# One core, attention then a squared-ReLU layer: the last queries' scores move into the half-row run, P.V joins the layers' PSUM ring, and more units of layer 1 are done by seven products

## The chip, the core and the metric

The kernel runs on one core of a Trainium2 chip. The time is the device time of the whole program in microseconds, one launch. A run of the kernel can also be profiled: the profile gives the span from the first to the last instruction, and the start and duration of every instruction on each engine. The engines are TensorE (PE; its weight loads are PEld), VectorE (DVE), ScalarE (ACT), GpSimd (POOL) and SyncE (SP, which here only issues DMAs). Each follows its own list of instructions, in the program's order, and they meet by semaphores.

## The reference

Inputs: q, k, v of 8 batches, 8 heads, 576 positions, 64 dimensions each; a table of 32 distance buckets by 8 heads; w_in (512 x 2048) and w_out (2048 x 512). All float32.

```
scores = q @ k^T / 8 + bias[bucket(|i - j|), head]       # per batch and head
attn   = softmax(scores)                                  # over the keys
x      = (attn @ v), heads side by side                   # 4608 tokens x 512
out    = (relu(x @ w_in) ** 2) @ w_out                    # 4608 x 512
```

From a distance of 128 on the bucket is the same, so the bias is a constant there, which drops out of the softmax; the kernel multiplies only a band around the diagonal by exp(bias).

## The kernel before, in words

**Work and staging.** A pair is two heads of one batch: 32 pairs. Their transposed queries and keys lie in `qt` and `kt` (fp16), head 0 of the pair on partitions 0 to 63, head 1 on 64 to 127. Positions 0 to 511 are four tiles of 128; 512 to 575 are the last 64. `pair` (from line 902) does a pair:

- The main scores, `run` (line 962): for each key tile `jt` and each head a product of 64 rows (the head's dimensions) by 512 queries into a bank of its own of the set `st` (two banks, one per head). Head 0 uses the upper half of TensorE's rows, head 1 the lower half; these are the products of line 971. Two sets exist (`r_set`), and ACT takes the exponential of a whole set (line 984, 1024 elements) into `pt`.
- The last keys, `last_keys` (line 1014): the 64 last keys of both heads against all queries. The keys of the two heads are spread into a zeroed block of 128 by 128 (`kz`), so that one full-row product serves both heads (line 1022).
- The last queries, `last_queries` (line 989): the 64 last queries of both heads spread in the same way into `qz` by four copies per pair (line 954, on POOL, in the first batches partly DVE); four full-row products of 128 columns, one for each key tile (line 997; line 854 in batch 0), into half a set, and one exponential of 512 elements (line 1007; 864).
- DVE multiplies the bands (line 710), then P.V in `values` (from line 722): per query tile one product with the last keys (line 736) and eight of 65 columns (line 743), into the single bank of the ring `r_pv`; DVE takes reciprocals and scales (757, 762), and SP transposes the result by DMA into `xt` (line 777). In batches 0 and 1 TensorE does that transposing (line 1089).

Batch 0 is done by halves of the queries (`half_of_pair`, line 788; scores at line 809, exponentials at 819, last keys at 832 and 841) so that layers can start early.

**Layers.** Tokens go in nine groups of 512. Layer 1 of a group is 16 blocks of 128 of w_in's columns: four products of 512 columns each (line 1486; in group 0 by halves of the tokens, line 1439), a ReLU on ACT (1515) and a square on DVE (1525). Layer 2 (`second`) is done for every group by seven products of blocks in place of eight (Strassen's way, line 1215); DVE makes the sums of activations (1170) and fuses the evacuations of the products (1243), ACT copies some (1249), SP stores (1271). For some blocks of layer 1 `by_sevens` does the same: a unit is four of the 16 blocks at once, seven products of four matmuls of 256 columns (line 1370), evacuated by ACT (1401) for products 1 and 2 and by fused additions on DVE (1396) for the other five, with ReLU (1410) and square (1419 on ACT or 1421 on DVE). It needs sums of w_in (per unit) and of x (per group), made by DVE in `late_sums` (line 1296). The sums of w_in are put in a `pt` buffer, `late["room"]`, that the attention no longer uses. `UNITS` says how many units a group has: one in group 7, two in group 8.

**PSUM.** Eight banks: two sets of two (`r_set`), one for P.V (`r_pv`), three for the rest (`r_g`: layers, transposes, tables). A use takes a buffer from a ring and gives it back when its last reader is done.

**Order.** The order is not that of the code. Each step is an `Op` with engine, cost, inputs, buffers and a due time; `Plan.schedule` (lines 187 to 270) places at each moment the op that can start first, and among those the one due first. The table `DUES` overwrites due times by an op's number, so it holds for one list of ops only. `mode` is "r" for the half-row runs, "c" for the transposes of line 927 and "f" for full-row work; the planner charges TensorE for a change of mode.

Of the kernel before, what the change touches and what calls it, by code (L numbers as in the profile page):

```python
# [22 lines left out]
HQ = 288  # L23
# [17 lines left out]
SIX = 2  # L41
V_EARLY, V_HW = 18900.0, 2
LATE2 = 7000
UNITS = {7: 1, 8: 2}
# [22 lines left out]
0:6314 10:217026 16:13035 20:13348 21:258484 25:16976 56:-3806 60:10549 64:7807 66:10391 72:10797 74:9599  # L67
80:12958 82:13335 86:9426 88:22059 90:20784 96:15474 98:18110 100:27635 102:17069 104:20413 106:19133 108:15929
110:20294 112:11373 114:26373 118:23163 120:26863 122:27399 124:27420 126:43949 128:373644 130:37551 132:55933
140:51535 146:53249 148:57194 150:58550 152:59093 154:59407 156:62212 158:60024 162:61598 164:73576 166:62626  # L70
168:69684 170:59456 172:62632 174:65227 176:55548 182:127159 185:61268 197:113382 198:91426 200:94475 202:78241
204:62718 208:77636 228:78221 232:79984 234:88997 236:93444 258:97082 260:107098 264:95693 272:353255 290:132179
294:109389 312:161034 317:126634 462:185572 468:197791 498:216177 504:216419 528:-11357 540:58268 548:290781
552:-273 556:362102 569:117287 570:18693 572:322613 573:269880 577:216286 580:63789 588:19830 590:16140
594:14836 595:13461 604:192461 605:259149 615:250357 618:40193 621:36476 626:164336 627:19259 631:22289
632:61824 637:27216 640:23193 641:22984 642:25439 646:24359 648:23862 654:35487 655:137994 656:25970 657:147534
658:26859 669:32802 670:29693 671:29115 675:26812 678:61416 684:27758 687:32723 692:45873 693:44475 694:33461
700:29155 703:40767 706:43870 707:156896 712:138157 715:49177 721:51431 727:42451 730:41204 733:51304 736:188811
739:160633 741:60556 745:65841 746:65543 750:23359 752:198955 754:252034 755:87356 757:149452 759:161491
764:165691 772:38120 780:31226 786:44132 789:65256 791:41900 794:47703 798:179998 803:183900 804:201524  # L80
806:29768 808:32093 814:128297 817:38985 819:48235 822:13166 831:74297 834:41254 836:42214 847:56558 872:76658
876:81357 881:86779 885:82175 890:132194 892:78033 896:74640 901:77029 905:85179 910:92737 913:136934 921:-441
928:71969 932:86010 949:99012 964:77998 968:82501 971:73188 973:72043 979:88379 993:74328 994:172863 1011:91462
1016:95167 1034:90187 1037:94214 1061:98210 1066:103404 1085:116705 1089:123193 1094:115422 1098:123870
1105:125413 1109:116922 1114:123206 1117:104913 1118:108524 1126:215561 1127:140015 1134:341379 1138:129625
1149:123522 1156:126934 1159:128458 1174:117297 1178:116128 1183:123079 1184:121785 1193:130123 1197:131687
1210:103421 1213:171180 1215:111597 1218:107124 1224:123395 1234:97893 1238:106935 1239:113870 1242:121817
1245:107498 1247:139583 1250:140247 1256:140312 1264:152762 1302:164129 1307:159578 1311:156509 1314:140955
1322:175554 1327:174839 1336:155878 1340:158933 1342:162590 1347:179715 1351:176523 1358:154680 1362:174863
1365:164726 1369:178450 1372:164377 1375:183307 1391:148354 1396:141354 1405:158959 1423:158387 1426:145359  # L90
1428:154083 1460:162604 1493:305936 1511:188689 1515:208724 1518:185439 1520:203719 1524:203903 1527:183718
1531:64671 1534:35571 1535:192349 1540:192734 1544:215992 1547:197129 1549:206804 1552:201055 1553:198295
1560:216382 1567:22170 1571:213455 1575:214781 1579:220037 1582:216714 1585:209292 1589:218699 1604:51306
1609:177927 1612:165312 1615:244855 1616:185704 1636:180272 1639:191978 1641:180694 1668:199141 1673:209138
1676:207232 1684:113822 1687:219314 1700:201270 1701:203032 1703:191761 1708:195625 1724:230338 1733:225496
1736:226874 1737:226114 1740:65884 1747:238275 1753:233568 1762:229606 1766:238797 1773:230961 1777:231038
1784:245369 1788:237869 1795:246877 1798:236767 1817:211479 1818:211996 1836:232334 1849:219048 1852:216620
1854:244560 1857:216881 1881:227052 1884:224715 1886:230825 1887:234567 1889:218551 1895:248220 1896:246247
1916:239890 1932:255715 1937:245391 1946:276466 1950:271723 1957:144182 1961:262946 1966:264120 1969:283402
1970:252823 1973:283834 1975:263020 1986:281169 1997:277541 2001:273225 2008:269557 2011:263820 2030:290375  # L100
2033:300439 2035:288262 2038:298147 2070:215597 2094:283860 2099:280265 2140:278987 2160:322023 2175:327834
2187:203430 2191:314100 2194:95297 2196:320960 2200:327640 2205:312307 2209:311170 2216:306662 2220:44915
2227:316413 2231:323176 2238:310309 2241:322560 2256:323083 2258:322318 2260:298171 2281:330645 2283:323528
2290:323454 2298:283980 2316:319108 2342:324427 2349:318937
# [146 lines left out]
def mm(n):  # L251
    return n / 2.4 + 2.5
# [11 lines left out]
def kernel(  # L264
# [44 lines left out]
    z_sb = sb("qz", [128, NQK, 2, 128])  # L309
    qzs, kzs = ([z_sb[:, i, w, :] for i in range(NQK)] for w in range(2))  # L310
# [19 lines left out]
    pv_ps = [psum.tile([128, 512], FP32, name=f"pv{i}") for i in range(1)]  # L330
    g_ps = [psum.tile([128, 512], FP32, name=f"f{i}") for i in range(3)]

    P = Plan()
    r_set, r_pv, r_g, r_lane = Ring(2), Ring(1), Ring(3), Ring(8)
# [136 lines left out]
    z_fix = [[fill(zz[:, 0], 0.0, 158.0, 10, QUIET)], [fill(zz[:, 1:], 0.0, 452.0, 11, LATER)]]  # L471
# [316 lines left out]

    def half_of_pair(p, part, turned):
# [10 lines left out]
        def scores(jt):  # L800
            st = Buf(r_set)

            def score():
                kt, qt = kts[qb.slot], qts[qb.slot]
                for j in range(2):
                    for e in range(2):
                        rw = ds(64 * e, 64)
                        io(
                            nc.tensor.matmul(  # L809
                                sets_ps[st.slot][:, e, ts(j, 256)], kt[rw, ts(jt + j, 128)], qt[rw, ds(q0, 256)],  # L810
                                start=True, stop=True,
                            )
                        )

            o = P.add({"PE": 2 * mm(256) + 10}, score, evac + ready, [st, qb, pb], T, 0.0, "r")

            def ex():
                io(
# [3 lines left out]
                    )  # L822
                )

            exps[jt] = P.add({"ACT": act(1024)}, ex, [o], [st, pb], T)

        def last_keys():
            st = Buf(r_g)
# [47 lines left out]
        if part:  # L876
            last_queries()
# [716 lines left out]
```

## Time and profile before

| | us |
|---|---|
| runs without profile | 365.94, 365.03, 367.13; median 365.94 |
| the profiled execution's own time | 365.5 |
| its span, first to last instruction | 363.7 |
| TensorE clock granted, mean | 1.00 |
| main scores, exponentials (ACT L984, L819) | 108.6 and 16.9 busy |
| last queries: products (L997, L854) | 10.7 and 1.6 busy, 128 matmuls |
| last queries: exponentials (L1007, L864) | 17.2 and 3.2 busy, 32 instructions |
| copies into qz and kz on POOL (L954) | 19.7 and 19.9 busy, 56 each |
| layer 1 in full blocks (L1486) | 113.8 busy, 592 matmuls |
| layer 1 by seven products (L1370) | 84 matmuls of 256 columns, 273 ns each |
| fused evacuations of these (DVE L1396) | 15 instructions, about 686 ns each |

A busy time is the union of the durations on an engine; a matmul's duration includes its way through the array, so that matmuls in sequence overlap, and what one takes of the stream is the distance from its start to the next start. In a group row of the profile the columns are line, engine, operation, out<-in, shape, count, busy time and mean ns. A row of TensorE's wait list is: who waited, for whom, total us, times, longest us. In a timeline row: start in us, duration in us of what is merged in the row, engine, line, operation, out<-in, shape, count.

### The profile page before, as it was taken

Reading aid. Unit: us, or ns where it says so; the run is one execution under the profiler, and the core shown is the slowest. Engines: PE = TensorE matmul, PEld = TensorE weight load, DVE = VectorE, ACT = ScalarE, POOL = GpSimd, SP = SyncE. Lnnn points to the kernel's source line nnn. Section 1 sums busy time; section 2 is a strip of 40 time slices with the busy share of each in tenths; the row PEclk is TensorE's granted clock in tenths of the full one; section 3 lists DMA queues with packets and bytes.
Section 4 is the critical chain, followed back from the end, with each engine's and each line's share of the span. In section 5 each row is a group of like instructions: output and inputs, shape, how many; then the busy total and the mean of one; then the engine's idle time right before and its main releaser. Section 6 shows DMA issues by size and latency. Waiting matters only on the chain.

```text
span 363.7 us, 10232 instructions
## 1 busy us (share of the span) xinstructions
PE 352.8 (97%) x4062; PEld 252.7 (69%) x4062; DVE 269.7 (74%) x622; ACT 260.1 (72%) x385; POOL 187.9 (52%) x345
## 2 busy tenths in 40 slices
PE   3989999999999999999999999999999999999996
PEld 2658787765687457777776566458777788566885
DVE  4889999767965598467687589558767685489683
ACT  4999998489866897588968787884685741667530
POOL 7998489979999989856777773012000000000000
PEclk9999999999999999999999999999999999999999
DMA  9999999999999999999999997234320132000032
GB/s 169 137 159 198 201 165 189 123 159 185 148 150 170 212 168 171 136 174 161 146 142 154 176 113 93 65 62 72 105 63 3 50 78 78 29 29 2 31 116 89
DMA packets 162256, 44.29 MB, mean 122 GB/s; under 512 B 145664, under 2 KB 162208, under 8 KB 162208
## 3 DMA queue, kind: packets, MB, share of 16 engines
q0 software_dynamic: 74208, 14.53, 51.4%
q1 hardware_dynamic: 87696, 28.80, 44.2%
q8 instruction: 32, 0.52, 0.6%
q10 hardware_dynamic: 304, 0.31, 0.3%
q14 instruction: 16, 0.13, 0.1%
HBM read 36.89 MB, written 9.44 MB: 127 GB/s over the span
## 4 chain that ended last, share of the span: by engine, by line
PE 92%; ACT 2%; DVE 0%; issue 0%
PE f L1215 30%; PE f L1486 28%; PE pv L743 10%; PE st L971 8%; PE f L1439 4%; PE pv L736 3%; PE st L1022 2%; PE st L997 2%; ACT pt L819 2%; PE st L1370 1%; PE pv L1370 1%; PE f L1089 1%; PE f L927 1%; PE pv L1215 0%; PE f L1370 0%; PE st L809 0%
## 5 line engine op out<-in xcount | busy, mean ns | idle before, releaser
L984 ACT ACTIVATE pt<-st 128x1024 f16<-128x1024 f32 x112 | 108.6, 1024 | 24.6 <-PE st L971 24.6
L1486 PE MATMUL f<-xt,w_in_sb 128*128 128x512 f16 (+4 forms) x592 | 113.8, 333 | 0.0
L1515 ACT ACTIVATE rt<-f 128x512 f16<-128x512 f32 x116 | 68.2, 606 | 31.6 <-PE f L1486 28.4
L1486 PEld LDWEIGHTS <-w_in_sb 128*128 128x128 f16 x592 | 51.8, 98 | 42.4 <-issue 9.8
L710 DVE TENSOR_TENSOR pt<-pt,tb_sb 128x512 f16<-128x512 f16 (+3 forms) x108 | 61.3, 580 | 18.1 <-ACT pt L984 16.5
L1525 DVE TENSOR_TENSOR g<-rt 128x512 f16<-128x512 f16 x116 | 50.6, 442 | 26.5 <-ACT rt L1515 25.0
L1215 PEld LDWEIGHTS <-g 128*128 128x128 f16 x576 | 54.6, 98 | 9.0 <-issue 2.1
L349 POOL DMA_DIRECT2D ks<-in_k_dram x79 | 55.9, 722 | 3.7 <-issue 1.2
L349 POOL DMA_DIRECT2D qs<-in_q_dram x79 | 55.5, 711 | 2.4 <-DMA qt<-qs 1.9
L743 PE MATMUL pv<-va,pt 128*128 128x65 f16 x1280 | 54.6, 193 | 0.0
L743 PEld LDWEIGHTS <-pt 128*128 128x128 f16 x1280 | 50.2, 97 | 2.0
L1215 PEld LDWEIGHTS <-s 128*128 128x128 f16 x432 | 40.8, 98 | 9.4 <-issue 4.2
L1243 DVE SCALAR_TENSOR_TENSOR y<-f,y 128x512 f32<-128x512 f32 (+1 forms) x47 | 31.3, 665 | 18.9 <-PE f L1215 16.8
L954 POOL COPY qz<-qt 64x64 f16<-64x64 f16 x56 | 19.7, 351 | 40.3 <-DMA qt<-qs 34.9
L1215 PE MATMUL f<-wt,g 128*128 128x256 f16 x288 | 36.2, 273 | 0.0
L1215 PE MATMUL f<-w_out_sb,s 128*128 128x256 f16 x288 | 35.8, 273 | 0.0
L736 PE MATMUL pv<-vm,pm 128*128 128x130 f16 x160 | 35.5, 222 | 0.0
L971 PE MATMUL st<-qt,kt 64*128 64x512 f16 x224 | 33.9, 381 | 0.0
L1215 PE MATMUL f<-w_out_sb,g 128*128 128x256 f16 x272 | 33.3, 273 | 0.0
L762 DVE TENSOR_TENSOR x<-pv,r 128x384 f16<-128x384 f32 (+1 forms) x64 | 31.1, 487 | 1.1
L954 POOL COPY qz<-kt 64x64 f16<-64x64 f16 x56 | 19.9, 356 | 10.4 <-DMA kt<-ks 4.8
L1170 DVE TENSOR_TENSOR s<-g,s 128x1024 f16<-128x1024 f16 x36 | 24.9, 697 | 0.1
(101 smaller groups left out, 412.2 us busy)
## 6 DMA issues: line engine op xcount, KB each, us to landing
out_dram<-y SPq DMA_DIRECT2D x34, 256.0 KB, 2.7
f<-in_v_dram SPq DMA_DIRECT2D x24, 256.0 KB, 4.6
ks<-in_k_dram POOLq DMA_DIRECT2D x48, 64.0 KB, 5.2
qs<-in_q_dram POOLq DMA_DIRECT2D x48, 64.0 KB, 4.7
w_in_sb<-in_moe_w_in_dram POOLq DMA_DIRECT2D x4, 512.0 KB, 8.7
w_out_sb<-in_moe_w_out_dram POOLq DMA_DIRECT2D x4, 512.0 KB, 13.0
ks<-in_k_dram POOLq DMA_DIRECT2D x7, 144.0 KB, 5.0
qs<-in_q_dram POOLq DMA_DIRECT2D x7, 144.0 KB, 4.8
```

The source lines that it names most:

```text
L349: lambda: io(eng.dma_start(out=out_(), in_=in_())),
L710: io(nc.vector.tensor_tensor(out=a, in0=a, in1=t, op=MULT))
L736: nc.tensor.matmul(ps[:, i, :, :], pm[:, c : c + 128], vm[:, hp, :, 0:65], start=True, stop=False)
L743: nc.tensor.matmul(ps[:, i, e, :], pt[:, (2 * jt + e) * S + c : (2 * jt + e) * S + c + 128], va[:, jt, 2 * hp + e, 0:65], start=False, sto ...
L954: io(eng.tensor_copy(out=dst[qb.slot][rw, rw], in_=src[qb.slot][rw, 512:576]))
L971: nc.tensor.matmul(sets_ps[st.slot][:, e, :], kt[rw, ts(jt, 128)], qt[rw, 0:512], start=True, stop=True,)
L984: nc.scalar.activation(out=p5(pts[pb.slot])[:, jt, :, 0:512], in_=sets_ps[st.slot], func=EXPF, scale=SCALE)
L1215: nc.tensor.matmul(home[bf.slot][:, ts(s_, HALF)], left(c, s_), right(c), start=(c == 0 and (s_ == 0 or apart) and (own or i not in before ...
L1243: nc.vector.scalar_tensor_tensor(out=dst, in0=ps, scalar=OSC, in1=ys[y[plus].slot][:, cs], op0=MULT, op1=mybir.AluOpType.add,)
L1486: nc.tensor.matmul(g_ps[bank.slot][:, a:z], w_in_sb[:, kk, ts(nt, 128)], xt_sb[:, kk, c : c + z - a], start=(kk == 0), stop=(kk == 3),)
L1515: io(nc.scalar.activation(out=rts[rb.slot], in_=g_ps[bank.slot], func=RELUF))
L1525: nc.vector.tensor_tensor(out=gs[gb1.slot][:, nt, :], in0=rts[rb.slot], in1=rts[rb.slot], op=MULT)
```

## The change

The last queries' scores are no longer four full-row products. `scores_of` puts them into the half-row run of the last key tiles (`run(..., True)`; in batch 0 the second half's `scores(2, True)`): eight products of 64 columns on half the rows, four for head 0 ahead of the large products, four for head 1 behind them, each head into a bank of its own from the ring `r_g`. Within the run head 1 now comes before head 0. `exp_of_last` takes two exponentials of 256 elements. `qz` and its copies are gone. The P.V bank joins the three others: `r_pv` is `r_g`, a ring of four banks. `UNITS` becomes three units in group 7 and four in group 8, so `by_sevens` uses two rooms. The table of due times is new throughout, so the order changes everywhere; among the first instructions SP now issues the bucket table before id and q, the cast of q is done by ACT, not DVE, and the small table product stands before the first transposes. In the changed program the lines are moved: half-row products 801 (64 columns) and 810, their exponentials 820 and 986 (853 in batch 0), P.V 740 and 747, layer 2 1193, seven products 1348, full blocks 1464.

```diff
--- before.py
+++ after.py
@@ -41,7 +41,7 @@
-UNITS = {7: 1, 8: 2}
+UNITS = {7: 3, 8: 4}
...
@@ -306,8 +310,8 @@
-    z_sb = sb("qz", [128, NQK, 2, 128])
-    qzs, kzs = ([z_sb[:, i, w, :] for i in range(NQK)] for w in range(2))
+    z_sb = sb("kz", [128, NQK, 128])
+    kzs = [z_sb[:, i, :] for i in range(NQK)]
@@ -327,11 +331,11 @@
-    pv_ps = [psum.tile([128, 512], FP32, name=f"pv{i}") for i in range(1)]
-    g_ps = [psum.tile([128, 512], FP32, name=f"f{i}") for i in range(3)]
+    g_ps = pv_ps = [psum.tile([128, 512], FP32, name=f"f{i}") for i in range(4)]
...
-    r_set, r_pv, r_g, r_lane = Ring(2), Ring(1), Ring(3), Ring(8)
+    r_set, r_g, r_lane = Ring(2), Ring(4), Ring(8)
+    r_pv = r_g
@@ -468,7 +472,7 @@
-    z_fix = [[fill(zz[:, 0], 0.0, 158.0, 10, QUIET)], [fill(zz[:, 1:], 0.0, 452.0, 11, LATER)]]
+    z_fix = [[fill(zz[:, 0], 0.0, 110.0, 10, QUIET)], [fill(zz[:, 1:], 0.0, 270.0, 11, LATER)]]
@@ -786,6 +790,42 @@
                 xt_ready.setdefault(g_, []).append(t)
         return o
 
+    def scores_of(slot, banks, jts, q0, n, lq):
+
+        kt, qt = kts[slot], qts[slot]
+        rw = [ds(64 * e, 64) for e in range(2)]
+
+        def last(e):
+            for j in range(4 if lq else 0):
+                io(
+                    nc.tensor.matmul(
+                        lq[e][:, ts(j, 64)], kt[rw[e], ts(j, 128)], qt[rw[e], 512:S], start=True, stop=True
+                    )
+                )
+
+        last(0)
+        for i, jt in enumerate(jts):
+            for e in (1, 0):
+                io(
+                    nc.tensor.matmul(
+                        banks[i][:, e, :], kt[rw[e], ts(jt, 128)], qt[rw[e], ds(q0, n)], start=True, stop=True
+                    )
+                )
+        last(1)
+
+    def exp_of_last(lq, pb, o, T):
+
+        def ex(e):
+            io(
+                nc.scalar.activation(
+                    out=p5(pts[pb.slot])[:, :, e, 512:S],
+                    in_=g_ps[lq[e].slot][:, 0:256].rearrange("p (j s) -> p j s", j=4),
+                    func=EXPF, scale=SCALE,
+                )
+            )
+
+        return [P.add({"ACT": act(256)}, lambda e=e: ex(e), [o], [lq[e], pb], T) for e in range(2)]
+
     def half_of_pair(p, part, turned):
 
         hp = p % 4
@@ -797,22 +837,16 @@
...
-        def scores(jt):
+        def scores(jt, last=False):
             st = Buf(r_set)
+            lq = [Buf(r_g) for _ in range(2)] if last else []
 
             def score():
-                kt, qt = kts[qb.slot], qts[qb.slot]
...
-            o = P.add({"PE": 2 * mm(256) + 10}, score, evac + ready, [st, qb, pb], T, 0.0, "r")
+                banks = [sets_ps[st.slot][:, :, ts(j, 256)] for j in range(2)]
+                scores_of(qb.slot, banks, [jt, jt + 1], q0, 256, [g_ps[x.slot] for x in lq])
+
+            took = 2 * mm(256) + 10 + (4 * mm(64) if last else 0)
+            o = P.add({"PE": took}, score, evac + ready, [st, qb, pb] + lq, T, 0.0, "r")
...
             exps[jt] = P.add({"ACT": act(1024)}, ex, [o], [st, pb], T)
+            if last:
+                exps["q"], exps["q1"] = exp_of_last(lq, pb, o, T)
@@ -834,7 +870,7 @@
-            o = P.add({"PE": mm(nk)}, score, evac + ready + spread[2:4], [st, qb, pb], T, 0.0, "f")
+            o = P.add({"PE": mm(nk)}, score, evac + ready + spread, [st, qb, pb], T, 0.0, "f")
@@ -845,36 +881,9 @@
...
         scores(0)
         last_keys()
-        scores(2)
-        if part:
-            last_queries()
+        scores(2, part == 1)
@@ -945,7 +954,7 @@
-        for w, src, dst in ((0, qts, qzs), (1, kts, kzs)):
+        for w, src, dst in ((1, kts, kzs),):
@@ -959,22 +968,15 @@
-        def run(jts):
+        def run(jts, last=False):
             sets = [Buf(r_set) for _ in jts]
+            lq = [Buf(r_g) for _ in range(2)] if last else []
 
             def score():
-                kt, qt = kts[qb.slot], qts[qb.slot]
...
-            o = P.add({"PE": len(jts) * mm(512) + 10}, score, evac, sets + [qb, pb], T, after, "r")
+                scores_of(qb.slot, [sets_ps[st.slot] for st in sets], jts, 0, 512, [g_ps[x.slot] for x in lq])
+
+            took = len(jts) * mm(512) + 10 + (4 * mm(64) if last else 0)
+            o = P.add({"PE": took}, score, evac, sets + [qb, pb] + lq, T, after, "r")
@@ -987,31 +989,8 @@
...
-        def last_queries():
-            st = Buf(r_set)
...
-                    io(
-                        nc.tensor.matmul(
-                            sets_ps[st.slot][:, 0, ts(jt, 128)], kts[qb.slot][:, ts(jt, 128)], qzs[qb.slot],
...
-            o = P.add({"PE": 4 * mm(128)}, score, evac + spread[0:2], [st, qb, pb], T, after, "f")
...
-            exps["q"] = P.add({"ACT": act(512)}, ex, [o], [st, pb], T)
+            if last:
+                exps["q"], exps["q1"] = exp_of_last(lq, pb, o, T)
-            o = P.add({"PE": 2 * mm(HQ)}, score, evac + spread[2:4], [st, qb, pb], T, after, "f")
+            o = P.add({"PE": 2 * mm(HQ)}, score, evac + spread, [st, qb, pb], T, after, "f")
@@ -1042,12 +1021,11 @@
             run([1])
             last_keys()
             run([2])
-            run([3])
+            run([3], True)
         else:
             run([0, 1])
             last_keys()
-            run([2, 3])
-        last_queries()
+            run([2, 3], True)
@@ -1063,7 +1041,7 @@
-                [exps[3], exps["q"]] + tabs_done[0:5], [pb], T,
+                [exps[3], exps["q"], exps["q1"]] + tabs_done[0:5], [pb], T,
@@ -1285,7 +1263,8 @@
     late = {}
 
     def sum_of_w(i, u):
-        return pts[late["room"].slot][:, ts(i - 1, 1024)].rearrange("p (k c) -> p k c", k=2)[:, :, ts(u, 256)]
+        room = pts[late["room", u // 2].slot][:, ts(i - 1, 1024)]
+        return room.rearrange("p (k c) -> p k c", k=2)[:, :, ts(u % 2, 256)]
 
     def late_sums(n, dst, terms, deps, due, bufs=()):
 
@@ -1303,10 +1282,9 @@
 
     def by_sevens(g, units, due):
 
-        assert max(UNITS.values()) <= 2
-        if not late:
-
-            late["room"] = Buf(r_pt)
+        for u in range(units):
+            if ("room", u // 2) not in late:
+                late["room", u // 2] = Buf(r_pt)
         c = (g * GT) % XR
         assert c + GT <= XR
         wq = lambda i, k, u: w_in_sb[:, 2 * k : 2 * k + 2, 1024 * i + 256 * u : 1024 * i + 256 * u + 256]
@@ -1335,7 +1313,7 @@
                         (4, (lambda u=u: wq(0, 1, u), lambda s_=s_: s_(2), SUB)),
                         (3, (lambda u=u: wq(0, 0, u), lambda u=u: wq(1, 0, u), SUB)),
                     ],
-                    l_win + last_scores, due + 10.0 * u, [late["room"]],
+                    l_win + last_scores, due + 10.0 * u, [late["room", u // 2]],
                 )
             banks = {"a": Buf(r_set), "b": Buf(r_g), "c": Buf(r_pv), "d": Buf(r_set)}
             y = {"u": Buf(r_f), "v": Buf(r_y)}
```

The table `DUES` (some 40 lines of numbers) is replaced as a whole and is not shown.

## The prediction

> **What bounds the kernel now.** I read the page first, then the list of what TensorE waited for, then its timeline, to price one instruction of each kind. The page's busy time and its slices:
>
> ```profile
> PE 352.8 (97%) x4062; PEld 252.7 (69%) x4062; DVE 269.7 (74%) x622; ACT 260.1 (72%) x385; POOL 187.9 (52%) x345
> PE   3989999999999999999999999999999999999996
> ACT  4999998489866897588968787884685741667530
> ```
>
> TensorE is full from the fourth slice on; ScalarE (ACT) is full only in slices 2 to 6. The waits of TensorE, all but one more of 0.3 us (L809, for DVE's kt):
>
> ```profile
> PE f L927 <- ACT ks L551: 5.2, 1, 5.2
> PE st L809 <- ACT pt L819: 1.0, 3, 0.5
> PE f L401 <- DMA g<-c_rep: 0.9, 1, 0.9
> PE st L809 <- ACT qt L696: 0.3, 1, 0.3
> ```
>
> The lines are all of the start (L809 is batch 0). After 28.7 us nothing is waited for, so there a change is worth what it does to TensorE's own stream, as long as it makes no new wait. Busy time overlaps, so the stream is priced by starts, in the timeline (start, duration):
>
> ```profile
> 76.72 1.03 PE L1486 MATMUL f<-xt,w_in_sb 128*128 128x512 f16 x4
> 77.67 0.61 PE L971 MATMUL st<-qt,kt 64*128 64x512 f16 x4
> 78.21 1.90 PE L1486 MATMUL f<-xt,w_in_sb 128*128 128x512 f16 x8
> ...
> 86.97 0.41 PE L743 MATMUL pv<-va,pt 128*128 128x65 f16 x8
> 87.21 0.22 PE L736 MATMUL pv<-vm,pm 128*128 128x130 f16 x1
> ...
> 90.62 0.39 PE L997 MATMUL st<-qz,kt 128*128 128x128 f16 x4
> 90.85 1.03 PE L1486 MATMUL f<-xt,w_in_sb 128*128 128x512 f16 x4
> ```
>
> and later, around the one seven-product group:
>
> ```profile
> 319.08 0.60 PE L1370 MATMUL f<-ks,pt 128*128 128x256 f16 x4
> 319.52 1.89 PE L1486 MATMUL f<-xt,w_in_sb 128*128 128x512 f16 x8
> 321.25 0.60 PE L1370 MATMUL f<-ks,pt 128*128 128x256 f16 x4
> ```
>
> From start to start: 128x512 costs 216 ns ((321.25-319.52)/8), 256 columns 109 ns, 128 columns 56 ns (0.23/4), the 65-column products of P.V 30 ns (0.24/8). A run on half the rows (L971) does 4x512 two by two, so 432 ns of streaming, in 0.54 us: about 0.1 us is lost at its end, and 0.09 at its start (0.95 for 4x216=864 ns before it). I take 97 ns per switch between the half-row and full-row forms. Adding these prices over the program's order gives 347.2 us; the profile's time minus this sum is 11.6 us at 29.7 us and 13.3 at the end: fill at the start, then 1.7 us of rounding, no stall. The span is 11.6 + 347.2 + 1.7 + 3.2 (tail: last evacuation and store). The profiled execution took 365.5 us (span 363.7), 0.4 below the shown median of 365.94.
>
> **Last queries.** The 4 products of 128 columns per pair (L997, L854) go: 128 x 56 = 7.2 us. In come 8 of 64 columns per pair, inside the last half-row run: four for head 0 first, then the large ones, head 1 before head 0, then four for head 1. No row shows 64 columns on half the rows. Nearest is L743, 65 columns with a new weight load each, 30 ns; I take 29. What a pair then costs depends on whether head 1's 512-column product may start while head 0's four are still queued. The Trainium skill speaks with two voices. Its page "TensorEngine Tiling (Array Packing)", Tiling Modes, says that different tiles execute loads and matmuls in parallel; then only 4x29 = 117 ns are added, as both halves carry equal work. Its page "TensorE: Matmul & The Clock Gate", Part 3, says that matmuls start and end strictly in program order; then head 1's product starts only with head 0's fourth, 87 ns late, and its own four come after at 4x29: 204 ns added. The row (L971, heads issued in turn) allows both. I take the in-order reading, as the timeline shows no start out of order: 32 x 204 = 6.5 us in, 7.2 out, -0.6 us; side by side it would be 3.7 in, -3.4 us.
>
> A rule of the Trainium skill speaks against short products: "TensorEngine Tiling (Array Packing)", Instruction Overhead, gives each matmul some 60 cycles. Read as added to the stream it is 25 ns on top of 27, 52 a piece, and 7x52 = 364 ns per pair: +4.5 us. The L743 row, 30 ns for 65 columns, says that it isn't added. I keep 29.
>
> ScalarE gets two exponentials of 256 elements for one of 512. Rows of batch 0:
>
> ```profile
> 15.77 0.41 ACT L841 ACTIVATE pm<-f 128x256 f16<-128x256 f32 x1
> 16.03 0.69 ACT L696 ACTIVATE kt<-f 128x576 f16<-128x576 f16 x1
> ...
> 23.35 0.78 ACT L864 ACTIVATE pt<-f 128x512 f16<-128x512 f32 x1
> 23.83 3.05 ACT L819 ACTIVATE pt<-st 128x1024 f16<-128x1024 f32 x3
> ```
>
> Start to start 0.26 against 0.48 us: +0.05 per pair, 1.6 us in all, hidden behind TensorE after the start (ACT is 72% busy); uncovered it would cost 1.6. The qz copies (64, mostly POOL at 0.35 us) and half the zero fill go at no gain on the path: only ACT's exponentials waited for qz, and TensorE did not wait for ACT. POOL's loads may run earlier; nothing waits for them.
>
> **Switches.** Counted in both built programs' orders, form changes on TensorE go from 154 to 149: 5 x 97 = -0.5 us.
>
> **Seven products.** Four more units: 64 products of 512 columns go (13.8 us), 112 of 256 come (12.2): -1.6 us, if TensorE stays the bound there. The stage before:
>
> ```profile
> 290.00:335.00 45.00, 45.00 (x382) 32.52 (x379) 33.01 (x71) 22.68 (x39) 0.00 (x0) 1.00 0.16 45
> ```
>
> The columns after TensorE and its loads are DVE 33.0 and ACT 22.7 of 45 us. In the new order, from the first of the seven units to product 1 of the last layer-2 group TensorE's stream is 39.7 us. DVE has 35 fused evacuations in it (5 a unit, 0.605 start to start in L1396), 16 sums and stores of layer 2 at 0.60 and 6 short ones at 0.34: 32.8 us. ACT has 35 copies and ReLUs (0.49 to 0.52) and 26 squares (0.53) with two copies more: 32.6 us. Both fit, with 7 us to spare, but each engine takes its instructions in the program's order, so I laid out this stage's DVE queue instruction by instruction against TensorE's sum (0.2 us from a product to its evacuation): every bank is free 0.3 to 0.6 us before its next product; the last squares land 0.35 us before product 1 of the last group. No stall, little margin; ends for the cost: -0 and +3 us. The 8 extra sums of w_in (8 x 0.34 on DVE) stand in front of that stage beside TensorE's layer 2, and so do the input's DMA transposes, which DVE's sums wait for; the last must be issued by SP behind two stores, and I find it landing some 2 us early.
>
> **Ring of four.** P.V, layer 1, layer 2 and the last queries now share four banks. In the order, the nearest reuse of a bank after last queries is 0.98 us of TensorE work later, the chain that frees it (end of the product 0.16, hand-over 0.04, exponential 0.43, hand-over 0.05) 0.68. Cost 0; bounds under rivals.
>
> **Start.** SP now loads q last, and q's cast moves to ACT behind the table's exponential; the table product stands before the first transposes, so TensorE begins with the wait for c_rep (6.7 us) in place of the one at 5.2. Following the queues, the first large exponential still starts near 10.6 us (10.73 before), as casts, tables and evacuations held it. From there ACT is the bound until the last batch-0 scores: its rows sum to 20.6 us up to the exponential that frees the set for the next last-keys product, so 31.2 us, where TensorE's sum stands at 20.6. Profile time less sum is then 10.6, against 11.8 before at that place (35.8 us). I count -0.7 of these -1.1, for small gaps on ACT; ends -1.5 and +1.0 (q's landing decides).
>
> **Sum.** -0.6 - 0.5 - 1.6 - 0.7 = -3.4 us: 362.1 against the profiled 365.5, 362.5 against the median.
>
> **Rivals.** (A) as summed, 362.5, chance 0.48. (B) The two halves run side by side: 2.8 us more gained, 359.7, chance 0.25. For it: the Tiling page, and that loads of both heads start 2 ns apart; against: the in-order rule. (C) ACT or DVE falls behind in the seven-product stage or early batches, 2 to 4.5 us of waits: about 365.7, no change, 0.14. For: ACT and DVE at 82% there, margins of 0.3 us; against: the same tightness caused no wait before. (D) Slower: a bank wait at the head of the last-queries run. Head 0's bank must be free before the first product, and behind it in TensorE's queue stand the large scores that feed ACT. If an ACT instruction (0.49 us) lies between, the run waits for it; at half of 32 runs that is 7.8 us: 370.3. It decides from a mean wait of 0.11 us per pair (gain gone), 0.16 for slower by 0.5%. For: three such waits in the start's L809 lines; against: none later. 0.09. (E) Short products at 52 ns: 367.6, 0.04; even at 44 ns.
>
> **Numbers.** Faster by over 0.5% (about what a measurement of this kernel can tell from no change, 1.8 us): A, B and a little of C, 0.75; within: 0.14; slower: 0.11. Range 358.9 to 366.2: from B with its better start to the middle of C; D, E and C's end stay out.
>
> **What would show it.** Last-queries lines of TensorE: the first large product of the run 90 ns after the first short one, and the short tail after it, show A; at once shows B. TensorE's waits after 30 us should be empty; an entry with "ACT pt" or "DVE x" at the short products shows D, one at the seven-product line C. DVE in 290 to 330 us near 85%. TensorE's 36 us mark should lie about 1 us deeper in its work. Wrong if the start's first exponential comes over 1 us late.

## The result, and the profile after

The changed kernel takes 363.68 us (median of 8 runs, 362.59 to 364.83), the kernel before 365.86 in the same set: ratio 0.9937, interval 0.992 to 0.9955, so 2.2 us less where 3.4 were forecast. Two later sets gave 0.9893 (0.9852 to 0.9934) and 0.9935 (0.9905 to 0.9965). The profiled execution took 364.48 us with a span of 362.7, 0.8 above its median; that of before took 365.5 with 363.7. The page's row of busy times and TensorE's slices, after the change:

```profile
PE 348.1 (96%) x4238; PEld 261.1 (72%) x4238; DVE 276.7 (76%) x624; ACT 271.1 (75%) x435; POOL 173.3 (48%) x293
PE   2887999999999999999999999999999999999996
```

TensorE is full later than before: its first four slices read 2, 8, 8, 7 where they read 3, 9, 8, 9. The list of its waits after the change:

```profile
PE f L405 <- DMA g<-c_rep: 6.9, 1, 6.9
PE st L810 <- DVE kt L702: 1.1, 1, 1.1
PE f L801 <- DVE qt L702: 0.9, 1, 0.9
PE f L1417 <- DMA w_in_sb<-in_moe_w_in_dram: 0.9, 1, 0.9
PE f L747 <- DMA va<-in_v_dram: 0.6, 1, 0.6
PE f L740 <- ACT pt L820: 0.4, 1, 0.4
...
PE f L1193 <- ACT y L1227: 0.2, 1, 0.2
```

All but the last lie before 36 us (left out is one of 0.3 us, there too). The last is a wait for a bank of the new ring: at 60.2 us a product of layer 2 stands until ACT has emptied a bank (it reads nothing that ACT writes). A second one, at 144.6 us (P.V, until DVE has emptied a bank), is too short for the list. By the starts they cost 0.22 and 0.25 us. Rival C's waits in the seven-product stage would show at L1348 and rival D's, all through, at L801; there are none. C's other place, the early batches, does have waits: 1.1 and 0.9 us at L810 and L801 for DVE, and 0.4 us at L740 for ACT's short exponentials. The last-queries run, in the timeline of TensorE:

```profile
172.77 0.20 PE L801 MATMUL f<-qt,kt 64*128 64x64 f16 x1
172.78 0.39 PE L810 MATMUL st<-qt,kt 64*128 64x512 f16 x1
172.81 0.25 PE L801 MATMUL f<-qt,kt 64*128 64x64 f16 x3
172.89 0.59 PE L810 MATMUL st<-qt,kt 64*128 64x512 f16 x3
173.22 0.28 PE L801 MATMUL f<-qt,kt 64*128 64x64 f16 x4
173.43 0.23 PE L740 MATMUL f<-vm,pm 128*128 128x130 f16 x1
```

Head 1's large product starts 13 ns after head 0's first short one, although three short ones stand ahead of it in the program; they start after it. Only the second four, at the end, take time. From the run's start to the next full-row product it is 665 ns (median), where a run of four large products takes 538: +126 ns a pair with rounding. That is rival B. The stage of the seven products, to be set beside the row from 290 us on that the prediction shows (columns: window, length, then busy time and instructions of TensorE, its loads, DVE, ACT, POOL, then clock and DMA):

```profile
290.00:335.00 45.00, 45.00 (x443) 39.02 (x441) 40.79 (x80) 29.24 (x53) 0.00 (x0) 1.00 0.18 54
```

DVE is at 40.8 of 45 us, and still TensorE is full. Time less the sum of prices stays level over the stage (17.4 us at 290, 17.5 at 350), so nothing stalls there.

**Where the gain went.** With 126 ns a pair the stream's prices fall from 347.2 to 341.9 us, by 5.2 before rounding. The span fell by 1.0. Of the difference 3.7 us are lost by 44 us (time less sum 15.5 there, 11.8 before), 0.5 in the two waits for banks. Two stretches of the start, before and then after the change:

```profile
16.00:32.00 16.00, 14.49 (x267) 10.68 (x264) 14.85 (x48) 16.00 (x26) 15.27 (x27) 1.00 1.51 171
32.00:44.00 12.00, 12.00 (x198) 9.79 (x195) 11.17 (x33) 11.17 (x19) 5.88 (x19) 1.00 1.32 202
```

```profile
16.00:32.00 16.00, 13.49 (x274) 10.27 (x269) 13.90 (x43) 15.71 (x29) 13.66 (x22) 1.00 1.40 153
32.00:44.00 12.00, 10.18 (x187) 8.12 (x186) 9.40 (x25) 9.88 (x17) 7.67 (x23) 1.00 1.33 200
```

Nearly 2 of the 3.7 us lie after 32 us, where before there was no wait. DVE's rows and TensorE's there, after the change (in brackets the idle time before the row and who ended it):

```profile
33.27 0.43 DVE L1123 TENSOR_TENSOR wt<-w_out_sb 128x512 f16<-128x512 f16 x1 [1.82 <-DMA w_out_sb<-in_moe_w_out_dram]
33.61 0.75 DVE L702 COPY qt<-f 128x576 f16<-128x576 f16 x1
```

```profile
34.42 0.27 PE L801 MATMUL f<-qt,kt 64*128 64x64 f16 x4 [0.95 <-DVE qt L702]
...
35.91 1.92 PE L1417 MATMUL f<-xt,w_in_sb 128*128 128x256 f16 x16 [0.87 <-DMA w_in_sb<-in_moe_w_in_dram]
```

A sum of w_out (L1123) stands in DVE's queue ahead of a query copy and waits 1.82 us for its weights; the copy waits behind it, and TensorE for the copy. Then TensorE waits for the second quarter of w_in, which POOL now issues after the first quarter of w_out (landing at 35.87 us; before, issued ahead of it, at 31.19).

Behind both stands POOL's own queue. A load from POOL holds one of eight lanes (`r_lane`) until it has landed. The first quarter of w_in landed at 21.68 us, and the next load that needed its lane, one of keys, held POOL's queue for 1.21 us:

```profile
22.23 0.63 POOL L353 DMA_DIRECT2D ks<-in_k_dram  x1 [1.21 <-DMA w_in_sb<-in_moe_w_in_dram]
```

The first quarter of w_out and the second of w_in stood behind it in that queue.

### The profile page after: what moved, and what is told of

Its sections match the earlier page's. It is cut to its first block, busy times and chain, and to the rows that moved or that the text cites. A ratio compares the mean times of both kernels' runs of the same rounds, so it can differ in the third digit from the quotient of the medians.

```text
span 362.7 us, 10596 instructions
## 1 busy us (share of the span) xinstructions
PE 348.1 (96%) x4238; PEld 261.1 (72%) x4238; DVE 276.7 (76%) x624; ACT 271.1 (75%) x435; POOL 173.3 (48%) x293
## 4 chain that ended last, share of the span: by engine, by line
PE 86%; DMA 6%; POOL 2%; DVE 2%; issue 1%; ACT 1%; POOLq 0%
PE f L1193 30%; PE f L1464 24%; PE f L747 9%; PE st L810 7%; DMA w_in_sb<-in_moe_w_in_dram 5%; PE f L1417 4%; PE st L1348 3%; PE f L740 3%; PE f L1348 3%; PE f L801 2%; PE st L1001 2%; DMA qs<-in_q_dram 2%; POOL va L353 1%; DVE s L1148 1%; ACT pt L986 1%
## 5 line engine op out<-in xcount | busy, mean ns | idle before, releaser
L986 ACT ACTIVATE pt<-st 128x1024 f16<-128x1024 f32 x112 | 111.0, 1031 | 25.4 <-PE st L810 19.1
L1464 PE MATMUL f<-xt,w_in_sb 128*128 128x512 f16 (+4 forms) x528 | 94.8, 328 | 0.0
L1464 PEld LDWEIGHTS <-w_in_sb 128*128 128x128 f16 x528 | 46.5, 98 | 35.8 <-issue 4.2
L1493 ACT ACTIVATE rt<-f 128x512 f16<-128x512 f32 x100 | 58.6, 613 | 17.9 <-PE f L1464 16.7
L1503 DVE TENSOR_TENSOR g<-rt 128x512 f16<-128x512 f16 x100 | 43.3, 445 | 18.7 <-ACT rt L1493 17.7
L747 PE MATMUL f<-va,pt 128*128 128x65 f16 x1280 | 53.6, 193 | 0.6 <-DMA va<-in_v_dram 0.6
L810 PE MATMUL st<-qt,kt 64*128 64x512 f16 (+1 forms) x288 | 43.4, 362 | 1.5 <-DVE kt L702 1.1
L963 POOL COPY kz<-kt 64x64 f16<-64x64 f16 x59 | 21.5, 365 | 42.7 <-DMA kt<-ks 23.1
L740 PE MATMUL f<-vm,pm 128*128 128x130 f16 x160 | 35.5, 222 | 0.5 <-ACT pt L820 0.4
L766 DVE TENSOR_TENSOR x<-f,r 128x384 f16<-128x384 f32 (+1 forms) x64 | 30.8, 486 | 1.0 <-DVE r L761 0.2
L820 ACT ACTIVATE pt<-f 128x256 f16<-128x256 f32 x64 | 23.1, 402 | 2.3 <-PE f L801 2.2
## 6 DMA issues: line engine op xcount, KB each, us to landing
w_in_sb<-in_moe_w_in_dram POOLq DMA_DIRECT2D x4, 512.0 KB, 10.6
```

Source lines behind the costliest of these rows:

```text
L740: nc.tensor.matmul(ps[:, i, :, :], pm[:, c : c + 128], vm[:, hp, :, 0:65], start=True, stop=False)
L747: nc.tensor.matmul(ps[:, i, e, :], pt[:, (2 * jt + e) * S + c : (2 * jt + e) * S + c + 128], va[:, jt, 2 * hp + e, 0:65], start=False, sto ...
L766: nc.vector.tensor_tensor(out=xs[xb.slot][:, qt0 : qt0 + nq, :].rearrange("p t (e d) -> p t e d", e=2), in0=ps[:, :, :, 0:64], in1=rs[rb.s ...
L810: nc.tensor.matmul(banks[i][:, e, :], kt[rw[e], ts(jt, 128)], qt[rw[e], ds(q0, n)], start=True, stop=True)
L986: nc.scalar.activation(out=p5(pts[pb.slot])[:, jt, :, 0:512], in_=sets_ps[st.slot], func=EXPF, scale=SCALE)
L1464: nc.tensor.matmul(g_ps[bank.slot][:, a:z], w_in_sb[:, kk, ts(nt, 128)], xt_sb[:, kk, c : c + z - a], start=(kk == 0), stop=(kk == 3),)
```

## The experiments

"After" is the changed kernel, and an experiment's edit is against it. "Ninth run" is the start of the ninth last-queries run in TensorE's timeline: 77.66 us in after, a mark of what the start lost.

**Short products doubled** (e1).

```diff
-            for j in range(4 if lq else 0):
+            for j in (0, 1, 2, 3, 0, 1, 2, 3) if lq else ():
```

> The changed kernel with each of the eight 64-column products of a last-queries run issued twice (the second writes the same numbers again), 256 products more in all. Theory, row halves run side by side and a short product costs its half 29 ns: four more on each half, 4 x 29 = 117 ns a pair, 32 pairs, +3.7 us on 363.7, so 367.4. Rival, read in order (the prediction's own sum, 204 ns for eight): +6.5 us, 370.2. Second rival, the short products lie beside other work anyway: no change, 363.7.

Measured 369.26 us, ratio to before 1.0078 (1.005 to 1.0107), 5.2 us above after by the ratios: between the two. The trace says more: the run grew from 665 to 902 ns, 237 and not 117 a pair, which over 32 pairs is 7.6 us (the profiled execution, 370.92 us, is the slowest of its four runs, and the ratio of after moved by 1.6 us between sets):

```profile
176.13 0.32 PE L801 MATMUL f<-qt,kt 64*128 64x64 f16 x5
176.26 0.39 PE L810 MATMUL st<-qt,kt 64*128 64x512 f16 x1
176.28 0.25 PE L801 MATMUL f<-qt,kt 64*128 64x64 f16 x3
176.37 0.59 PE L810 MATMUL st<-qt,kt 64*128 64x512 f16 x3
176.70 0.39 PE L801 MATMUL f<-qt,kt 64*128 64x64 f16 x8
```

Here the large product starts after the fifth short one (135 ns, not 13), again with three left to pass. The four extra ahead of it cost 122 ns, the four extra at the tail 116. So "side by side" without a bound fell: in these two kernels it holds only while no more than three waiting products must be passed.

**Large products exchanged** (e5), a test of that bound.

```diff
-            for e in (1, 0):
+            for e in (0, 1):
```

> The changed kernel with the two heads' large products of a run exchanged: head 0's large product, which has to wait for its own four short ones, now stands ahead of head 1's. The trace of the changed kernel has head 1's large product start 13 ns after the first short one, ahead of three short ones that stand before it in the program; in the doubled kernel it started only once five of eight had started, again with three left. Theory, a product can start ahead of at most three that still wait: here it starts one short product later (two started, three waiting), some 29 ns a pair, 32 x 29 = 0.9 us on 363.7, a run of about 690 ns for 665. Rival, strictly in order: 4 x 29 = 117 ns a pair, 3.7 us, a run of 780. Second rival, each row half takes its products with no bound on how many are passed: no change, 665.

Measured 364.02 us, ratio 0.9944 (0.991 to 0.9978), which can't resolve 0.9 us. The trace can: the run is 698 ns, 33 more (29 expected; strictly in order it would be some 780, without a bound 665).

```profile
171.60 0.23 PE L801 MATMUL f<-qt,kt 64*128 64x64 f16 x2
171.64 0.39 PE L810 MATMUL st<-qt,kt 64*128 64x512 f16 x1
171.66 0.22 PE L801 MATMUL f<-qt,kt 64*128 64x64 f16 x2
```

Two short ones start, then head 1's large product passes the two others and head 0's large one: three again.

**Doubled, heads in turn** (e6).

```diff
-        last(0)
+        for j in (0, 1, 2, 3, 0, 1, 2, 3) if lq else ():
+            for e in range(2):
+                io(
+                    nc.tensor.matmul(
+                        lq[e][:, ts(j, 64)], kt[rw[e], ts(j, 128)], qt[rw[e], 512:S], start=True, stop=True
+                    )
+                )
...
-        last(1)
```

> The doubled kernel again (each of the eight short products issued twice, the same numbers), but with the two heads' short products taking turns ahead of the large ones, so that the two row halves can run side by side without any product passing another. Theory, the 237 ns a pair that the first doubling added were the bound of three on passing, not the work: sixteen short products are 8 x 29 = 233 ns on each half, a run of about 780 ns for 665, +3.7 us, 367.4. Rival, the row halves don't share these products' time at all: sixteen in a row, the run stays at 902 ns as when doubled head by head, +7.6 us on the profiled time.

Measured 366.88 us, ratio 1.002 (0.9997 to 1.0043), +3.0 us (3.8 above the changed kernel in the same set, e8). The run is 771 ns, +106; sixteen short products pass in 0.24 us, two by two:

```profile
182.02 0.41 PE L801 MATMUL f<-qt,kt 64*128 64x64 f16 x16
182.26 0.60 PE L808 MATMUL st<-qt,kt 64*128 64x512 f16 x4
182.79 0.23 PE L740 MATMUL f<-vm,pm 128*128 128x130 f16 x1
```

The same work as in e1 takes 131 ns a pair less, by its order alone.

**Old share of seven products** (e2).

```diff
-UNITS = {7: 3, 8: 4}
+UNITS = {7: 1, 8: 2}
```

The due times of this stage were set anew.

> The changed kernel with only the old share of seven-product units: one in group 7 and two in group 8, as before the change; the due times of this stage are set anew. Theory, the 64 products of 216 ns taken out and 112 of 109 ns put in come straight off the end: giving them back costs 64 x 216 - 112 x 109 = 1.6 us, so 365.3. Rival, they are covered or the eviction engines delay the new units by as much: no change, 363.7. Second rival, the units stall for the eviction engines: giving them back gains, under 363.

Measured 365.04 us, ratio 0.9969 (0.9946 to 0.9991), +1.2 us by the ratios. From the last score product to the end it is 75.61 us against 74.07 in after, and 74.01 to 74.08 in e1, e3 and e4: +1.5 us for the 1.6 of the sum. Theory held, and both rivals fell.

**Two steps of the start moved** (e3). In the finished order the steps of a list are put ahead of a mark:

```diff
+MOVES = [
+    (None, [90], 114),
+    (None, [528, 529, 530, 531], 759),
+]
```

Step 90 loads the second quarter of w_in, 114 the first of w_out; 528 to 531 are its sums.

> The changed kernel with two steps of the start moved and nothing else: the second quarter of w_in is issued on POOL ahead of the first quarter of w_out (the order of the kernel before), and the four sums of the first quarter of w_out stand some 8 us later on DVE, behind the copies that the scores wait for. Theory, the stretch from 32 to 36 us lost 1.8 us of TensorE to these two (0.95 us behind a query copy that stood behind a sum, 0.87 us for the landing of w_in): -1.0 to -1.8 us, 361.9 to 362.7. Rival, the later quarters of w_in or ACT take the time back: 363.7.

Measured 363.22 us, ratio 0.9926 (0.99 to 0.9953), 0.4 us under after and not told apart from it. In its profiled execution both waits are gone, but TensorE then stands for 1.2 us until 38.3 us, for a load of keys that landed at 38.2; that is what the rival said. But this execution (366.13 us) is the slowest of its seven and lost up to 1.7 us at half clock from 17.4 to 20.8 us, so it doesn't tell what the others did. That the two steps are worth 1.0 us or more isn't shown, nor that landings take all of it back.

**The start's order set anew** (e4, e7).

```diff
+FIRST = """
...
+"""
+ON = {52: 'DVE', 547: 'ACT', 559: 'ACT', 565: 'DVE', 745: 'ACT', 743: 'DVE', 797: 'DVE'}
```

> The changed kernel with the order of its first 70 us set anew on every engine but the issue of loads (which keeps its order but for the second quarter of w_in ahead of the first of w_out); seven casts and copies change between ACT and DVE; the work is the same. Theory, the 3.7 us that the changed kernel's start lost against the kernel before came from the order in which its steps stand on DVE, ACT and TensorE: -1.5 to -3 us, 360.7 to 362.2. Rival, the start is bound by what ACT has to do and by landings, whatever the order: at most -0.5, 363.2 or more.

Measured 366.45 us, ratio 1.0001 (0.9986 to 1.0017): the gain was gone. A P.V product stood too early and waited 1.97 us for its bands, and then the granted clock (third column from the right) fell by half:

```profile
22.00:24.00 2.00, 1.67 (x22) 1.18 (x23) 0.70 (x3) 0.53 (x1) 1.59 (x3) 0.59 1.49 184
24.00:26.00 2.00, 2.00 (x35) 1.68 (x35) 1.02 (x5) 1.47 (x3) 2.00 (x3) 0.56 1.38 152
26.00:28.00 2.00, 2.00 (x46) 1.54 (x41) 1.65 (x6) 2.00 (x5) 2.00 (x4) 1.00 1.90 134
```

By half-microseconds it is 0.5 from 22.3 to 25.7 us: 3.4 us at half rate, up to 1.7 us lost beside the gap (an estimate: half of it). Thirteen of this kernel's 14 runs show a mean clock of 0.995 or less; the other took 365.93 us, so the half clock isn't the whole loss. A second wait of P.V for its bands, 1.25 us, stands at 68 us.

> The changed kernel with the order of its first 62 us set anew on every engine, the issue of loads included; eleven casts and copies change between ACT and DVE, the work is the same. It differs from the earlier reordered start in that no gap over 0.7 us is left on TensorE even if the landings come 2 us later. Theory, the earlier one failed by one gap of 2 us (a P.V product that waited for a v load and its bands), after which the granted clock stood at 0.56 to 0.59 for some 4 us: without it, 0.5 to 1.4 us under the changed kernel, 362.3 to 363.2. Rival, the start is bound by landings and ACT whatever the order: 363.7 or more.

Measured 368.18 us, ratio 1.0053 (1.0032 to 1.0074). The order found for it had the load of the first keys third on ACT's queue: it landed at 7.82 us (4.88 in after), and the first transposition began at 8.7 us (7.4), the first large exponential at 13.35 us (11.47). Gaps of 0.95 and 1.21 us were left on TensorE as well. The ninth run is at 78.73 us; less that delay of 1.9 us it would be near 76.8, no better than executions of the unedited start (75.0 to 77.7). So this kernel doesn't test its theory, and shows no gain from the order. In e4 two misplaced products cost 3.2 us of waits, in e7 the late load some 1.9 us, more than the theory had to win.

**The changed kernel again** (e8, e11) and **the kernel before again** (e12), without an edit.

> The changed kernel itself once more. Theory, of the 3.7 us that the start lost in its profiled execution a part was the landing times of that execution (the first quarter of w_in landed at 21.68 us there, and at 19.74 to 21.85 in others with the same order): the start to the ninth last-queries run, 77.66 us there, comes out up to 2 us earlier, and the ratio to the kernel before stays at 0.992 to 0.9955. Rival, the whole 3.7 us are the order of the steps: 77.4 to 77.9 again.

> The changed kernel once more, as the measure of this set for the edits to its front. Its two profiled executions had the ninth last-queries run at 77.66 and 75.01 us: theory, an execution's landing times decide within some 2.7 us, so a third lies in 75 to 78 us; the ratio to the kernel before 0.989 to 0.9955.

> The kernel before, once more, for a second profiled execution of its start. In the first the large products of the scores after the start kept their program order with 11.8 us of TensorE time lost by 44 us; theory, its landings vary as those of the changed kernel do and so does this loss, by up to 2.7 us; rival, only the changed kernel's order is open to them and it comes out within 0.5 us of 11.8. Ratio 1.

e8: 363.04 us, ratio 0.9893; ninth run at 75.01 us, 2.65 us earlier where up to 2 were expected, span 361.2. e11: 364.44 us, 0.9935; 77.21 us, as expected, span 363.1. e12: 366.42 us, 1.0 (0.9972 to 1.0028). The stretches of the start in e8, as shown of before and after above:

```profile
16.00:32.00 16.00, 13.94 (x278) 10.89 (x279) 14.70 (x46) 15.74 (x29) 14.07 (x25) 1.00 1.47 172
32.00:44.00 12.00, 11.77 (x214) 9.47 (x211) 10.51 (x29) 11.52 (x21) 7.26 (x21) 1.00 1.35 201
```

The program is the same as in after, but the first quarters of w_in and w_out landed at 19.26 and 30.69 us, not 21.68 and 33.25, and the two waits at 34 to 36 us don't occur. Not all of this is the loads' own time: from issue to landing the first took 5.85 us for 7.70, the second 7.39 for 8.01, and the rest is earlier issue. POOL didn't have to stand for the first quarter in e8; in e11, where it landed at 21.64, POOL stood 1.49 us. The start's loss against before is 3.7 us in after, 1.1 in e8, 3.3 in e11 (its clock was at 0.55 to 0.60 from 22 to 26 us, after a gap of 0.94 us). The kernel before is steadier: its second execution's marks (first and last L971) lie 0.5 us later than the first's. The theory that its start varies as much wasn't borne out by these two.

What stays in e8 points to the order: every execution of the unedited start has a wait of 0.9 to 1.1 us near 17 us for a key copy on DVE (0.3 before) and one of 0.4 us near 32 us where P.V waits for the short exponentials of batch 0 (none before). Together, less the 0.3, they come to some 1.2 us, about e8's loss. Nearly all of the other 2.6 us of after are three waits that e8 doesn't have: 0.6 us for a load of v at 22.3 us, which stands behind the first quarter of w_in on POOL, and the 0.9 and 0.9 us shown. Besides, e8 and e11 wait 1.0 and 0.9 us for a block of xt near 116 us, where neither execution of the kernel before waits; after doesn't either.

**The first 12 us put back** (e9), **and one transposing load moved besides** (e10).

```diff
+MOVES = [
+    (None, [4, 0], 10),
+    ('DVE', [52], 15),
+    (None, [546], 13),
+    (None, [547, 548, 549], 15),
+    (None, [544], 18),
+    (None, [572], 552),
+    (None, [1236], 1238),
+]
```

Only e10 has the last line. 4, 0 and 10 are the loads of id, q and table, 52 the cast of q, 546 and 544 transpositions, 547 to 549 copies, 572 the first scores; 1236 is a queries' load with a transpose, 1238 that of its keys, on SP with the stores into xt between them.

> The changed kernel with six steps of its first 12 us put back as the kernel before had them, and nothing else: on SP the identity and the q load ahead of the one-hot table, the q cast on DVE and not ACT, the transposition of the first keys ahead of the far product, the first copies and scores ahead of the table products. Theory, the late first exponential (11.47 us for 10.73 before; the prediction said 10.6) came from these steps and what ACT starts late it ends late: the first large exponential at about 10.7 us, the start 0.7 us shorter, 0.7 us off the time of the same kernel without the edit. Rival, landings and the later waits set the start's end: no change against the unedited kernel of the same set, whatever the first exponential does.

> As the kernel with the front put back, and besides one transposing load of queries is moved on SP's queue from ahead of two transposing stores into xt to behind them (near 107 us). Theory, the wait of 1.0 to 1.3 us on TensorE near 116 us (four products of layer 1 for the last block of xt, issued on SP behind that load; it shows in four of the nine executions seen) goes, and no other takes its place: no wait for xt over 0.3 us there, 0.5 us on average off the kernel with the front alone. Rival, the scores then wait for the queries' load: a wait of about 1 us for qt or kt near 118 us instead.

e9: 363.8 us, ratio 0.9924 (0.9894 to 0.9953); e10: 363.71 us, 0.9905 (0.9867 to 0.9943), beside e11's 364.44 and 0.9935 in the same set. TensorE begins at 5.3 and 5.1 us, not at 6.3 to 7.0, but the first large exponential only at 10.92 and 11.13 us (10.90, 11.47 and 11.59 unedited), so that part of the theory failed. The ninth run lies at 74.66 and 75.25 us, where five executions of the unedited start (after, e2, e5, e8, e11) gave 75.0 to 77.7. In both the first quarter of w_in landed early (19.1 and 19.4 us); beside the three unedited executions where it did too (75.0, 75.6 and 76.1, landing at 19.3 to 19.7) they are 0.6 us earlier on average. That leans towards the theory, but the intervals overlap, and six of e9's ten runs show a clock of 0.995. In e10 the wait for xt near 116 us, 1.0 us in e8 and 0.6 in e9, is gone and no other wait stands between 100 and 130 us, as the theory has it; but this is one execution, and of the nine seen before (the wait shows in five, 0.5 to 1.3 us) after and e5 are among those that lack it without the edit. The 0.5 us off e9 isn't shown (363.71 and 363.8 us). e10 has the shortest profiled span, 360.0 us; that it is faster than the changed kernel isn't shown.

## Why the prediction was nearly right

- **Last queries.** This step failed: "I take the in-order reading". The term was 204 ns a pair in; it measured 126, so -3.1 us, not -0.6. The price of 29 ns was right (and E's 52 wrong). The order reading was not: a product of the other row half started ahead of three that the program has first, so the run takes 665 ns, not 742. What the Trainium skill's page "TensorE: Matmul & The Clock Gate", Part 3, says of strict order doesn't hold here (13 ns, where order would give 87); what its page "TensorEngine Tiling (Array Packing)", Tiling Modes, says of tiles in parallel holds within the bound of three that e1, e5 and e6 show.
- **Seven products.** Right: -1.6 expected, 1.5 measured in e2, no stall. DVE was busy for 90% of 290 to 330 us, where near 85% was forecast, so the margin was thinner than laid out.
- **Switches.** -0.5, by the prices; not tested by itself.
- **Ring of four.** "Cost 0" was a little off: the two waits for banks cost 0.5 us. The exponentials of 256 cost 0.27 us each (two in 0.53), hidden but in batch 0, where P.V waited 0.4 us for them.
- **Start.** This step failed with the wrong sign: "I count -0.7" (of its -1.1, which by its own 10.6 and 11.8 is -1.2); 1.1 to 3.7 us were lost in three executions. The first exponential came at 11.47 us (10.90 to 11.59; 10.73 and 11.26 in the two executions of the kernel before), not 10.6; that was the smaller part. The step took ACT as the bound up to 31 us and looked no further, with the landings of the trace of before. It didn't ask what the new order on POOL and DVE does from 32 us on: a quarter of w_out ahead of a quarter of w_in, and sums of w_out ahead of a copy that scores wait for. Nor did it ask what a late landing does to POOL's queue, or which copy on DVE the scores near 17 us need. That the steps from 32 us on are a cause is read from the trace; e3, which moved them, gained no time that can be told.
- **The sum.** -5.2 in the stream instead of -2.7 and +1 to +4 at the start instead of -0.7 gave -2.2 for -3.4. Two errors of opposite sign made the total look better than its steps: that the total lies so near is luck.

Open: how much of the start's loss is order and how much the landing times of an execution. By the waits some 1.1 us is order, in every execution, and up to 2.6 more where the first quarter of w_in lands near 21.6 us and holds POOL; no experiment varied that landing or the lanes alone. e9 and e10 suggest that the front's order is worth some 0.6 us, within what the sets can't separate.

## What to carry to other kernels

Once TensorE is the bound, an order change is not free at the start: follow each queue until the last weight has landed, the queue that issues the loads too, and look for steps that wait for a late landing ahead of a copy that TensorE needs (what moving them is worth wasn't shown here). Row halves can hide small products, if no more than three waiting ones stand ahead of the product that should start; take the heads in turn where there are more. A start that depends on landings has to be judged by several executions, since one profile can be off by more than the change.

## What was not expected of the hardware

- TensorE starts products out of program order across row halves, in these kernels past three waiting ones at most (13 ns behind the first of four short ones, 135 ns behind the first of eight). So what is said above of all engines, that each follows the program's order, doesn't hold for these starts.
- A gap of 0.94 to 1.97 us on TensorE was followed by 3.4 us at half clock in e3, e4 and e11; gaps of 1.13 us in e8 and 1.56 us in e1 were not, so the length of the gap alone doesn't decide it. The Trainium skill's page "TensorE: Matmul & The Clock Gate", Part 1, has the half rate after an idle window of some 3.4 us; here the gap was much shorter. Of the kernel before, 4 of 103 runs show a mean clock of 0.995 or less, of the changed kernel 4 of 23, of e4 13 of 14.
- The same program's loads landed up to 2.6 us apart between executions (first quarter of w_out: 30.69 and 33.25 us). The load itself accounts for 0.6 us of that, its issue for 1.9; the first quarter of w_in took 5.85 and 7.70 us from issue to landing.
